# Turning two more batches of h on VectorE, moving their weights' low parts to GpSimd, and longer rows for the expert loads

## The chip, the cores and the metric

The kernel runs on one core of one Trainium2 chip. The metric is the device time of one execution in microseconds (us). The core has five engines with a queue each: TensorE (PE; its weight loads are listed apart as PEld), VectorE (DVE), ScalarE (ACT), GpSimd (POOL) and SyncE (SP), which issues all DMAs here. An engine takes its own queue in order.

## The reference, cut to what matters

Attention with normalised q and k feeds a gated feed-forward layer, and that feeds a soft mixture of experts. There are 4 batches of 448 tokens, 12 heads of 64, model width 768, hidden width 1536, 8 experts with 4 slots each and expert width 1024.

```
q_n, k_n = rmsnorm(q, g_q), rmsnorm(k, g_k)
attn = softmax(q_n @ k_n.T / 8);  x = (attn @ v), heads side by side        # 1792 x 768
h = silu(x @ w_gate) * (x @ w_val);  x2 = h @ w_out
logits = x2 @ phi                                   # 32 slots
slot_input = softmax over tokens(logits).T @ x2
slot_out[e] = relu(slot_input[e] @ w1[e]) @ w2[e]   # 8 experts, 50.3 MB of weights
out = softmax over slots(logits) @ slot_out
```

The kernel never forms x2. It uses w_out @ phi for the logits, and sums h over tokens with the slots' weights before it multiplies by w_out. For that sum h is needed with tokens on the partitions, while the feed-forward layer leaves it with hidden units on the partitions: each block of h (128 hidden units by 448 tokens) has to be turned. That turning is the subject here.

## The kernel before, in words

The program is a row of steps t. Steps 0 to 27 do the attention of batch 0 and prepare w_out @ phi. From step 28 on, u = t - 28 counts units of the feed-forward layer: 24 units for each batch, an even unit for a gate block and the odd one after it for the matching value block, 12 blocks of h a batch. Beside the units of batches 0, 1 and 2 run the scores and softmax of the attention of a later batch, four steps c = 0 to 3 for a pair of heads (three steps with two score tiles, the fourth with one). The units of batch 3 (u = 72 to 95) run without attention. Behind them come the slots' sums, the experts and the output.

Within a step the work is issued in the order of a table of names: ORD1 (line 1303) for batch 0, ORD2 (line 1306) for all later steps. Each engine gets its instructions in that order. The names that matter here, with the lines of the profile:

- S: scores of this step (L442, L446). M0, M1: their maxima on VectorE (L457). E0, E1: exponentials on ScalarE (L469). N0: the reciprocals of their sums on VectorE (L481, L482). N1, N2: scaling by them on GpSimd (L486). P0, P1: four transposes each of the step before's probabilities on TensorE (L521), and V0, V1 their copies out of PSUM (L535, L537). X: probabilities times v (L548). T, TH, L: transposes of the next q or k (L372), and their high and low parts (L403, L405, L414, L62). Q: on GpSimd the powers and products that normalise q and k (L340, L341, L347).
- G0, G1: the two halves of unit u, 9 matmuls each (L615), from a weight's high part wh and low part wl and x's high and low parts. WH makes wh of unit u+1 on ScalarE (L231); WL makes wl of unit u+1 by a subtraction (L239), in `w_lo`.
- AT, AM: the gate's and the value's activation (L629 on ScalarE, L636 and L642 on VectorE), which give the block ht of h.
- HT (`h_trans`, lines 658 to 674): turns a block by four TensorE transposes (L666) and one ScalarE copy (L670) into hn. Token chunks are 4 of 112 (`tok`, line 644). H0 to H3 (`h_squares`, lines 679 to 690): turn a block by 16 VectorE transposes of 32 by 32 squares (L685), four for each quarter of the block, H0 and H1 in the step after the block's value unit, H2 and H3 one step later. Here the chunks are 128, 128, 128 and 64 tokens, and the last chunk's lower half is set to zero by a GpSimd memset (L655). Before the change batches 0 to 2 use HT, and batch 3 uses H0 to H3.
- Z1, Z2, Z3, Z4: the slots' part of a finished batch, with the sums over h (`slots4`, L782) at u = 26, 50 and 74.

The low parts wl are made on VectorE for units 0 to 71 and on GpSimd (W4) for batch 3. The expert weights come in 32 units of 1.5 MB (`load_unit`): from u = 73 on, one load at every other step, and the rest behind the steps, each when its buffer comes free. Where a buffer is two half tiles, a unit is loaded in pieces (L940).

Of the kernel before, what the change touches and what calls it, by code (L numbers as in the profile page):

```python
# [21 lines left out]
def attn_moe_softmoe_kernel(  # L22
# [15 lines left out]
    nc = tc.nc  # L38
    B, H, S, HD = q.shape
    NT, DM = out.shape  # L40
    DFF = w_out.shape[0]
    NS = phi.shape[1]
    E, _, F = w1.shape
    SPE = NS // E
    P = 128
    CP = 112
    NC = S // CP
# [3 lines left out]
    KH = F // P  # L51
# [33 lines left out]
    ident = cpool.tile([P, P], F32, name="ident")  # L85
# [557 lines left out]

    def tok(b):

        return [P] * (S // P) + [S % P] if b == B - 1 else [CP] * NC

    def hn_tile(u):
        b, r = divmod(u, NU)
        g, f4 = divmod(r // 2, 4)  # L650
        d = bt[b]
        if g not in d["hn"]:
            d["hn"][g] = hnp.tile([P, NC, 512], F32, tag="hn", name="hn", bufs=3)
            if b == B - 1:
                nc.gpsimd.memset(d["hn"][g][S % P :, NC - 1], 0.0)  # L655
        return d["hn"][g], P * f4

    def h_trans(u, ht=None):

        b, r = divmod(u, NU)  # L660
        hn, o = hn_tile(u)
        ht = bt[b]["ht"][r // 2] if ht is None else ht
        th4 = pt_tile("th4")
        t0 = 0
        for c, n in enumerate(tok(b)):
            nc.tensor.transpose(th4[:n, P * c : P * c + P], ht[:, t0 : t0 + n], ident)  # L666
            t0 += n
        th4 = th4.rearrange("p (c f) -> p c f", c=NC)
        if b < B - 1:
            nc.scalar.copy(out=hn[:CP, :, o : o + P], in_=th4[:CP])  # L670
        else:
            n = S % P
            nc.scalar.copy(out=hn[:, : NC - 1, o : o + P], in_=th4[:, : NC - 1])
            nc.vector.tensor_copy(out=hn[:n, NC - 1, o : o + P], in_=th4[:n, NC - 1])

    SQ = 32
    hts_ = {}

    def h_squares(u, g):
# [76 lines left out]
    def slots3(b):  # L756
        d = bt[b]
        dp = pt_tile("dp")
        d["dn"] = mp.tile([P, NC, NS], F32, tag="dn", name="dn", bufs=1)
        if b == B - 1:  # L760
            nc.gpsimd.memset(d["dn"][S % P :, NC - 1], 0.0)

        for n, (src, dst, ck) in enumerate(((d["et"], d["dn"], tok(b)), (d["lr"], ce[:, b], [CP] * NC))):
            o = dp[:, NC * NS * n : NC * NS * (n + 1)].rearrange("p (c s) -> p c s", c=NC)
            t0 = 0
            for c, m in enumerate(ck):
                nc.tensor.transpose(o[:m, c], src[:NS, t0 : t0 + m], ident[:NS, :NS])
                t0 += m
            if n == 0 and b == B - 1:
                nc.vector.tensor_copy(out=dst[:, : NC - 1], in_=o[:, : NC - 1])  # L770
                nc.vector.tensor_copy(out=dst[: ck[-1], NC - 1], in_=o[: ck[-1], NC - 1])
            elif b < B - 1:
                nc.vector.tensor_copy(out=dst[:CP], in_=o[:CP])
            else:
                nc.scalar.copy(out=dst[:CP], in_=o[:CP])

    def slots4_mul(b, g):
        d = bt[b]
        sp = pt_tile("sp")
        n = P if b == B - 1 else CP  # L780
        for c in range(NC):
            nc.tensor.matmul(  # L782
                sp[NS * c : NS * c + NS, :], d["dn"][:n, c, :], d["hn"][g][:n, c, :], start=True, stop=True
            )
        return sp
# [135 lines left out]
    def load_unit(u):  # L921
        if u >= NE:
            return
        e, i, n = eunits[u]
        if i == 0:
            w, src = F, w1[e, KD2 * P * n : KD2 * P * (n + 1)].rearrange("(c p) f -> p c f", p=P)
        elif i == 1:
            w, src = DM, w2[e, KH2 * P * n : KH2 * P * (n + 1)].rearrange("(c p) f -> p c f", p=P)
        else:
            w, src = DM // 2, w2[e, :, DM // 2 * n : DM // 2 * (n + 1)].rearrange("(c p) f -> p c f", p=P)  # L930
        t = unit_tile(u)
        if isinstance(t, list):
            hf = KD2 * F // 2
            wtile[u] = lambda c, o, m: t[(c * w + o) // hf][:, (c * w + o) % hf : (c * w + o) % hf + m]
            for h in range(2):
                o = hf * h
                while o < hf * (h + 1):
                    c, lo = divmod(o, w)
                    m = min(w - lo, hf * (h + 1) - o)
                    nc.sync.dma_start(out=t[h][:, o - hf * h : o - hf * h + m], in_=src[:, c, lo : lo + m])  # L940
                    o += m
            return
        t = t.rearrange("p (c f) -> p c f", f=w)
        wtile[u] = lambda c, o, m: t[:, c, o : o + m]
        if u < NE - 1:
            nc.sync.dma_start(out=t, in_=src)
        else:
            for c in range(0, KH, 2):
                nc.sync.dma_start(out=t[:, c : c + 2], in_=src[:, c : c + 2])


    M0 = NP * NC + 4
# [2 lines left out]
    def wu(u):  # L955
        return NO + u if 0 <= u < B * NU else None
# [146 lines left out]
    def step(t):  # L1103
# [102 lines left out]

        def WL():
            if u + 1 < last:
                w_lo(wu(u + 1), nc.gpsimd if u + 1 < NU and WL1 == "p" else nc.vector)

        def M_(j):
            if att:
# [47 lines left out]
        def HT():  # L1260
            if prev is not None and prev % 2 == 1:
                if prev == B * NU - 1:
                    fill(LF[3])
                    slots1(B - 1)
                elif prev < (B - 1) * NU:
                    h_trans(prev)

        def H_(g):

            w = prev if g < 2 else u - 2  # L1270
            if w is not None and (B - 1) * NU <= w < B * NU - 1 and w % 2 == 1:
                if g == 0:
                    hts_[w] = bt[w // NU]["ht"][w % NU // 2]
                h_squares(w, g)
# [28 lines left out]
        "AT NB Z3 X W4 S NC XM NA SP T AM WH P0 Z1 TH G0 M0 M1 L WL E0 CT E1 N0 P1 XH R0 Z4 V1 HT N1 V0 XL N2 C SS G1 LG Q R Z2"  # L1303
    ).split()
    ORD2 = (
        "H2 H3 X S NB Z3 T AT NC M0 AM XM XH TH W4 M1 Z4 XL P0 V0 E0 L SP WH G0 NA Z1 CT E1 HT H0 H1 N0 R0 Z2 N1 N2 SS P1 G1 WL R LG V1 Q C"
    ).split()
    LF = [4, 3, 2, 0]
    LRE = 'v'
# [93 lines left out]
    with tc.manual_schedule():  # L1403
# [14 lines left out]
        sit_ps = pt_tile("sit")  # L1418
        for c in range(KD):
            nc.tensor.matmul(  # L1420
                sit_ps[:, NS * c : NS * c + NS], si[:, P * c : P * c + P], stack[:, 0, :], start=True, stop=True
            )
        sit = tp_.tile([P, KD, NS], F32, name="sit")
        nc.vector.tensor_copy(out=sit, in_=sit_ps[:, : KD * NS].rearrange("p (c s) -> p c s", c=KD))
# [34 lines left out]
        for u, (e, i, n) in enumerate(eunits):  # L1459
            w = wtile.pop(u)  # L1460
            if i == 0:
                if n == 0:
                    hacc[e] = s_tile(e % 3)[:, :FQ]
                for c in range(KD2 * n, KD2 * n + KD2):
                    for j in range(4):
                        nc.tensor.matmul(  # L1466
                            hacc[e][NS * j : NS * j + NS, :],
                            sit[:, c, :],
                            w(c % KD2, FQ * j, FQ),
                            start=(c == 0),  # L1470
                            stop=(c == KD - 1),
                        )
                if n == 1:

                    h1m = tp_.tile([P, KH, NS], F32, tag="h1m", name="h1m", bufs=2)
                    nc.gpsimd.memset(h1m, 0.0)
                    hr = tp_.tile([P, FQ], F32, tag="hr", name="hr", bufs=2)
                    nc.scalar.activation(out=hr, in_=hacc.pop(e), func=AF.Relu)
                    ht_ = pt_tile("htp")
                    for t in range(2):  # L1480
                        nc.tensor.transpose(ht_[:, P * t : P * t + P], hr[:, P * t : P * t + P], ident)
                    for t in range(2):
                        nc.vector.tensor_copy(
                            out=h1m.rearrange("p (j t) s -> p t j s", t=2)[:, t, :, SPE * e : SPE * e + SPE],
                            in_=ht_[:, P * t : P * t + P].rearrange("p (j s) -> p j s", j=4)[
                                :, :, SPE * e : SPE * e + SPE
                            ],
                        )
                    h1s[e] = h1m
            else:  # L1490
                for kh_ in range(KH2 * n, KH2 * n + KH2) if i == 1 else range(KH):
                    for j in range(4) if i == 1 else (2 * n, 2 * n + 1):
                        nc.tensor.matmul(  # L1493
                            so[NS * j : NS * j + NS, :],
                            h1s[e][:, kh_, :],
                            w(kh_ % KH2, DQ * j, DQ) if i == 1 else w(kh_, DQ * (j - 2 * n), DQ),
                            start=(e == 0 and kh_ == 0),
                            stop=(e == E - 1 and kh_ == KH - 1),
                        )
# [51 lines left out]
```

## Time and profile before

| | us |
|---|---|
| median of 3 runs | 825.45 (822.0 to 825.55) |
| the profiled execution | 825.7 |
| its span, first to last instruction | 823.9 |

The profiled execution is 0.25 us over the median. Beside the span lie 1.8 us. TensorE is busy 95% of the span, VectorE 59%, ScalarE 53%, GpSimd 47%. On the chain that ended last TensorE holds 85% and DMA 6%. Busy time shows what an engine does, and only the waits and the chain show whether it holds the others up; a busy TensorE is also not TensorE at its peak.

### The profile page before, as it was taken

The page shows a single profiled execution, that of the slowest core. Times are in us where ns is not written, and L with a number is a line of the kernel's source. Part 1 is how long each engine was busy: PE and PEld are TensorE (multiplying, and loading weights), DVE is VectorE, ACT ScalarE, POOL GpSimd, SP SyncE. Part 2 cuts the span into 40 slices and gives each one's busy share as a digit, 9 for nine tenths or more (in the row PEclk, how much of TensorE's full clock was granted, in tenths as well). Part 3 has the DMA queues.
Part 4 walks back from the last instruction along what each step waited for, and adds up shares of the span by engine and source line. Part 5 has one row for each costly group of instructions (what it writes and reads, how often), then busy time and mean ns, then how long its engine had stood idle before and what let it go on. Part 6 is the DMA issues. An engine that isn't in the chain of part 4 may idle for free.

```text
span 823.9 us, 14472 instructions
## 1 busy us (share of the span) xinstructions
PE 781.5 (95%) x5440; PEld 584.0 (71%) x5440; DVE 484.7 (59%) x943; ACT 434.8 (53%) x943; POOL 386.7 (47%) x354
## 2 busy tenths in 40 slices
PE   6899999999999999999999999999999999888676
PEld 5556657787778767877778677877878888555344
DVE  4879988777778555545555655544348778410013
ACT  3767887787778546655557465554432222211013
POOL 7988876665756444655355346422133445010000
PEclk8999999999999999999999999999999999999878
DMA  6556766675666312323232122221227888899998
GB/s 216 161 163 210 216 208 191 221 227 177 194 194 208 116 63 81 91 70 97 75 111 92 51 80 82 75 71 58 69 89 238 298 303 326 275 389 403 402 378 262
DMA packets 77892, 148.88 MB, mean 181 GB/s; under 512 B 5888, under 2 KB 48128, under 8 KB 77824
## 3 DMA queue, kind: packets, MB, share of 16 engines
q1 hardware_dynamic: 77824, 147.97, 53.9%
q8 instruction: 43, 0.70, 0.4%
q14 instruction: 25, 0.20, 0.1%
HBM read 128.29 MB, written 19.66 MB: 180 GB/s over the span
## 4 chain that ended last, share of the span: by engine, by line
PE 85%; DMA 6%; POOL 2%; ACT 2%; DVE 2%; issue 1%; SPq 0%; DVEq 0%; POOLq 0%; ACTq 0%
PE pg L615 43%; PE tp L521 9%; PE xp L548 7%; PE s L442 6%; DMA w<-in_moe_w_dram 6%; PE tq L372 3%; PE s L548 2%; PE th L666 2%; PE so L1493 2%; PE s L446 2%; PE lp L709 2%; PE sp L782 1%; PE s L1466 1%; PE s L1450 1%; PE tw L247 1%
## 5 line engine op out<-in xcount | busy, mean ns | idle before, releaser
L615 PE MATMUL pg<-xh,wh 128*128 128x448 f32 x576 | 224.1, 389 | 0.1
L615 PE MATMUL pg<-xl,wh 128*128 128x448 f32 x576 | 210.6, 366 | 0.0
L615 PE MATMUL pg<-xh,wl 128*128 128x448 f32 x432 | 157.6, 365 | 0.0
L457 DVE TENSOR_REDUCE sm<-s 128x1 f32<-128x448 f32 x168 | 100.7, 619 | 83.4 <-PE s L442 67.6
L486 POOL TENSOR_SCALAR pr<-pr,su 128x448 f32<-128x448 f32 x84 | 80.4, 966 | 139.9 <-ACT pt L535 62.5
L615 PEld LDWEIGHTS pg<-xh,wh 128*128 128x128 f32 x576 | 108.5, 188 | 15.3 <-issue 7.9
L615 PEld LDWEIGHTS pg<-xl,wh 128*128 128x128 f32 x576 | 108.8, 189 | 6.6 <-issue 0.2
L469 ACT ACTIVATE pr<-s,sm 128x448 f32<-128x448 f32 x168 | 107.6, 643 | 11.0 <-DVE sm L457 10.8
L535 ACT COPY pt<-tp 112x512 f32<-112x512 f32 x130 | 75.4, 590 | 66.0 <-PE tp L521 59.9
L521 PE MATMUL tp<-ident,pr 128*112 128x128 f32 x672 | 103.6, 277 | 2.5 <-ACT pt L535 1.8
L521 PEld LDWEIGHTS tp<-ident,pr 128*112 128x112 f32 x672 | 76.2, 134 | 29.3 <-issue 6.6
L231 ACT CAST wh<-raw 128x768 fp32r<-128x768 f32 x96 | 79.9, 835 | 23.8 <-POOL raw L239 23.6
L615 PEld LDWEIGHTS pg<-xh,wl 128*128 128x128 f32 x432 | 81.1, 188 | 6.7
L239 DVE TENSOR_TENSOR wl<-raw,wh 128x768 fp32r<-128x768 f32 x72 | 74.4, 1034 | 8.3 <-ACT wh L231 8.3
L239 POOL TENSOR_TENSOR raw<-raw,wh 128x768 fp32r<-128x768 f32 x24 | 44.2, 1842 | 69.3 <-ACT wh L231 67.1
L341 POOL TENSOR_TENSOR ri<-ss,mhalf 112x16 f32<-112x16 f32 (+1 forms) x25 | 72.8, 2911 | 2.1
L442 PE MATMUL s<-ka,qa 64*128 64x448 f32 x432 | 64.7, 404 | 0.8 <-ACT qa L403 0.7
L629 ACT ACTIVATE ht<-pg 128x448 f32<-128x448 f32 x48 | 26.1, 544 | 70.9 <-PE pg L615 45.9
L347 POOL TENSOR_TENSOR qn<-qk,ri 112x512 f32<-112x512 f32 x46 | 59.1, 1286 | 1.1
L548 PE MATMUL xp<-pt,vt 112*64 112x448 f32 x288 | 58.1, 545 | 0.0
L442 PEld LDWEIGHTS s<-ka,qa 64*128 64x128 f32 x432 | 35.5, 187 | 27.3 <-issue 24.3
L615 PE MATMUL pg<-xh,raw 128*128 128x448 f32 x144 | 52.8, 366 | 0.0
(162 smaller groups left out, 1153.0 us busy)
## 6 DMA issues: line engine op xcount, KB each, us to landing
w<-in_moe_w_dram SPq DMA_DIRECT2D x25, 1536.0 KB, 10.3
raw<-w SPq DMA_DIRECT2D x72, 384.0 KB, 3.2
w<-raw SPq DMA_DIRECT2D x36, 384.0 KB, 2.9
r<-in_moe_w_out_dram SPq DMA_DIRECT2D x12, 768.0 KB, 4.9
r<-in_moe_w_gate_dram SPq DMA_DIRECT2D x12, 768.0 KB, 5.1
r<-in_moe_w_val_dram SPq DMA_DIRECT2D x12, 768.0 KB, 5.1
qk<-in_q_dram SPq DMA_DIRECT2D x24, 224.0 KB, 2.9
qk<-in_k_dram SPq DMA_DIRECT2D x24, 224.0 KB, 3.2
```

Source lines behind the costliest of these rows:

```text
L231: (nc.vector.tensor_copy if u - NO < NU and WH1 == "v" else nc.scalar.copy)(out=wh, in_=wst[u]["raw"])
L239: eng.tensor_tensor(out=wl, in0=wst[u]["raw"], in1=wst[u]["wh"].bitcast(F32), op=ALU.subtract)
L341: nc.gpsimd.tensor_tensor(out=ri, in0=ss, in1=mhalf[:, : len(ns)], op=ALU.pow)
L347: eng.tensor_tensor(out=st[i]["qn"][:, n].rearrange("p c h d -> p h c d"), in0=st[i]["qk"][:, n], in1=st[i]["ri"][:, n] .rearrange("p (h c ...
L442: nc.tensor.matmul(sc[j], qa[r, wt, c * P : (c + 1) * P], ka[r, mv, :], start=(n == 0), stop=(n == 2))
L457: nc.vector.tensor_reduce(out=d["sm"][:, j : j + 1], in_=d["sc"][j], axis=AX.X, op=ALU.max, negate=True)
L469: nc.scalar.activation(out=p, in_=d["sc"][j], func=AF.Exp, bias=d["sm"][:, j : j + 1], accum_out=st[i]["su"][:, c, j : j + 1])
L486: nc.gpsimd.tensor_scalar(out=p, in0=p, scalar1=su[:, j : j + 1], scalar2=1.0, op0=ALU.mult, op1=ALU.mult)
L521: nc.tensor.transpose(tp[:CP, ck * P : (ck + 1) * P], pr[:, ck * CP : (ck + 1) * CP], ident)
L535: eng(out=st[i]["pt"][j][:, :, c * P : (c + 1) * P], in_=tp)
L548: nc.tensor.matmul(xp[HD * j : HD * j + HD, :S], d["vt"][:, j, ck, :], d["pt"][j][:, ck, :], start=(ck == 0), stop=(ck == NC - 1),)
L615: nc.tensor.matmul(d[r], wt[:, P * c : P * c + P], mv, start=(c == 0 and n == 0), stop=(c == KD - 1 and n == 2),)
```

## The change

Four edits. `SQB` is B - 3 = 1.

- Batches 1 and 2 are turned like batch 3: H0 to H3 in place of HT, with chunks of 128, 128, 128 and 64 tokens, and a memset for each of their hn tiles and the dn tile.
- The low parts wl of the units of batches 1 and 2 are made on GpSimd in place of VectorE.
- Expert loads: a partition takes 3 neighbouring rows of w1 (12288 bytes in one piece) in place of 3 pieces of 4096 bytes, or 2 neighbouring rows of w2 (6144 bytes) in place of pieces of 3072 bytes. Half tiles take 6144 bytes a partition. The last four units (halves of w2's columns, 1536 bytes a piece) keep their pieces, but all four, and not only the last, are issued in four parts of 384 KB. To match, the slots' sums (si) and the experts' hidden values (hr) are read with strides of 3 and 2 elements by the transposes.
- A new ORD2.

```diff
-        return [P] * (S // P) + [S % P] if b == B - 1 else [CP] * NC
+        return [P] * (S // P) + [S % P] if b >= SQB else [CP] * NC
...
-            if b == B - 1:
+            if b >= SQB:
                 nc.gpsimd.memset(d["hn"][g][S % P :, NC - 1], 0.0)
...
-    SQ = 32
+    SQ, SQB = 32, B - 3
...
-            w, src = F, w1[e, KD2 * P * n : KD2 * P * (n + 1)].rearrange("(c p) f -> p c f", p=P)
+            w, src = F, w1[e, KD2 * P * n : KD2 * P * (n + 1)].rearrange("(m p c) f -> p m (c f)", m=1, p=P)
         elif i == 1:
-            w, src = DM, w2[e, KH2 * P * n : KH2 * P * (n + 1)].rearrange("(c p) f -> p c f", p=P)
+            w, src = DM, w2[e, KH2 * P * n : KH2 * P * (n + 1)].rearrange("(m p k) f -> p m (k f)", p=P, k=2)
         else:
-            w, src = DM // 2, w2[e, :, DM // 2 * n : DM // 2 * (n + 1)].rearrange("(c p) f -> p c f", p=P)
+            w, src = DM // 2, w2[e, :, DM // 2 * n : DM // 2 * (n + 1)].rearrange("(m p k) f -> p m k f", p=P, k=2)
...
-                w_lo(wu(u + 1), nc.gpsimd if u + 1 < NU and WL1 == "p" else nc.vector)
+                w_lo(wu(u + 1), nc.gpsimd if u + 1 >= SQB * NU else nc.vector)
...
-                elif prev < (B - 1) * NU:
+                elif prev < SQB * NU:
                     h_trans(prev)
...
-            if w is not None and (B - 1) * NU <= w < B * NU - 1 and w % 2 == 1:
+            if w is not None and SQB * NU <= w < B * NU - 1 and w % 2 == 1:
...
-        "H2 H3 X S NB Z3 T AT NC M0 AM XM XH TH W4 M1 Z4 XL P0 V0 E0 L SP WH G0 NA Z1 CT E1 HT H0 H1 N0 R0 Z2 N1 N2 SS P1 G1 WL R LG V1 Q C"
+        "NB S R0 SS AT X WH NC T XM Z3 W4 AM XH TH M1 Z4 H0 M0 E0 XL H2 H1 SP L E1 Q H3 G0 P0 WL Z1 HT Z2 N0 G1 N2 NA CT P1 V1 LG R V0 N1 C"
...
-                sit_ps[:, NS * c : NS * c + NS], si[:, P * c : P * c + P], stack[:, 0, :], start=True, stop=True
+                si[:, KD2 * P * (c // KD2) : KD2 * P * (c // KD2 + 1)].rearrange("q (p c) -> q c p", c=KD2)[:, c % KD2],
...
-                        nc.tensor.transpose(ht_[:, P * t : P * t + P], hr[:, P * t : P * t + P], ident)
+                            ht_[:, P * t : P * t + P], hr.rearrange("q (p t) -> q t p", t=2)[:, t], ident
```

On TensorE, in a step c = 2 of batch 1 (scores s, transposed probabilities tp, unit pg, turned block th; nine pg rows make one half), before:

```order
L442 MATMUL s<-ka,qa 128x448 x6
L521 MATMUL tp<-ident,pr 112x128 x4
L615 MATMUL pg<-xh,wh 128x448
...
L666 MATMUL th_4131<-ident,ht 112x128 x4
L521 MATMUL tp<-ident,pr 112x128 x4
L615 MATMUL pg<-xh,wh 128x448
...
```

And the same step now:

```order
L442 MATMUL s<-ka,qa 128x448 x6
L615 MATMUL pg<-xh,wh 128x448
...
L521 MATMUL tp<-ident,pr 112x128 x4
L615 MATMUL pg<-xh,wh 128x448
...
L521 MATMUL tp<-ident,pr 112x128 x4
```

The four transposes of the h block are gone, and each set of transposed probabilities stands behind a half unit in place of ahead of it.

On GpSimd, the four steps of one pair of heads in batch 1 (qz is a copy of q's last columns, pr the probabilities, ri and qn the normalising, wl the low part), before:

```order
L423 COPY qz_110<-qa 64x2x64 x2
L486 TENSOR_SCALAR pr<-pr,su 128x448 x4
L340 TENSOR_SCALAR ss<-ss 112x16
L341 TENSOR_TENSOR ri<-ss,mhalf 112x16
L486 TENSOR_SCALAR pr<-pr,su 128x448 x2
L347 TENSOR_TENSOR qn<-qk,ri 112x2x4x64
L486 TENSOR_SCALAR pr<-pr,su 128x448
L347 TENSOR_TENSOR qn<-qk,ri 112x2x4x64
```

And now:

```order
L423 COPY qz_110<-qa 64x2x64 x2
L239 TENSOR_TENSOR wl<-raw,wh 128x768
L486 TENSOR_SCALAR pr<-pr,su 128x448 x2
L340 TENSOR_SCALAR ss<-ss 112x16
L341 TENSOR_TENSOR ri<-ss,mhalf 112x16
L239 TENSOR_TENSOR wl<-raw,wh 128x768
L486 TENSOR_SCALAR pr<-pr,su 128x448 x2
L347 TENSOR_TENSOR qn<-qk,ri 112x2x4x64
L239 TENSOR_TENSOR wl<-raw,wh 128x768
L486 TENSOR_SCALAR pr<-pr,su 128x448 x2
...
```

Four subtractions came in, each ahead of its step's scalings, and the power of step c = 1 (ri) and the products (qn) stand ahead of the subtraction.

On VectorE, the step c = 2 now (maxima sm, activation ht, squares hn, reciprocals su); before, neither the squares nor anything else stood between its two maxima but the activation, and a subtraction wl stood at its end:

```order
L642 SCALAR_TENSOR_TENSOR ht<-ht,pg 128x448
L457 TENSOR_REDUCE sm<-s 128x1
L685 STREAM_TRANSPOSE hn<-ht 32x4x32 x2
L685 STREAM_TRANSPOSE hn<-ht 32x3x32 x2
L457 TENSOR_REDUCE sm<-s 128x1
L685 STREAM_TRANSPOSE hn<-ht 32x4x32 x2
L685 STREAM_TRANSPOSE hn<-ht 32x3x32 x2
L481 TENSOR_SCALAR su<-su 128x2
L482 RECIPROCAL su<-su 128x2
```

Eight squares came in at this step, four of them between the two maxima.

## Rows read from the trace of the kernel before

**Rows 1.** The page, engines: busy us, share of the span, instructions.

```profile
PE 781.5 (95%) x5440; PEld 584.0 (71%) x5440; DVE 484.7 (59%) x943; ACT 434.8 (53%) x943; POOL 386.7 (47%) x354
```

**Rows 2.** Stretches: length, busy us (instructions) of PE, PEld, DVE, ACT, POOL; clock; DMA.

```profile
304.00:467.00 163.00, 162.24 (x975) 125.86 (x967) 90.48 (x174) 95.58 (x207) 81.40 (x79) 1.00 0.28 84
467.00:612.00 145.00, 144.99 (x849) 113.91 (x848) 70.59 (x132) 76.91 (x163) 50.19 (x51) 1.00 0.24 73
740.00:760.00 20.00, 17.82 (x334) 11.66 (x338) 0.77 (x6) 2.70 (x6) 1.79 (x5) 1.00 1.03 405
788.00:800.00 12.00, 9.27 (x96) 6.00 (x90) 0.61 (x3) 0.38 (x1) 0.00 (x0) 0.85 1.06 373
```

**Rows 3.** Waits of PE from 304 to 612 us: total, times, longest.

```profile
PE dp L767 <- DVE dn L773: 0.8, 1, 0.8
```

**Rows 4.** Chain in batch 1, order of time: start, us, what.

```profile
349.52 3.16 PE xp L548 x16
352.68 0.81 PE s L442 x6
353.48 0.53 PE tq L372 x4
...
354.45 1.83 PE pg L615 x9
...
361.77 0.44 PE th L666 x4
...
375.50 3.16 PE xp L548 x16
```

**Rows 5.** Groups from 304 to 612 us: busy us, mean ns; idle before.

```profile
L486 POOL TENSOR_SCALAR pr<-pr,su 128x448 f32<-128x448 f32 x73 | 70.4, 973 | 122.9 <-ACT pt L535 62.5 <-ACT hn L670 30.3 <-DVE su L482 30.0
L239 DVE TENSOR_TENSOR wl<-raw,wh 128x768 fp32r<-128x768 f32 x45 | 46.0, 1022 | 8.3 <-ACT wh L231 8.3
L457 DVE TENSOR_REDUCE sm<-s 128x1 f32<-128x448 f32 x73 | 45.4, 622 | 74.3 <-PE s L442 59.7 <-PE s L446 14.5
L341 POOL TENSOR_TENSOR ri<-ss,mhalf 112x16 f32<-112x16 f32 x9 | 26.3, 2919 | 0.8
L642 DVE SCALAR_TENSOR_TENSOR ht<-ht,pg 128x448 f32<-128x448 f32 x24 | 14.7, 612 | 4.9 <-PE pg L615 4.9
L327 DVE TENSOR_REDUCE ss<-qn 112x16 f32<-112x1024 f32 x8 | 9.6, 1199 | 0.0
L481 DVE TENSOR_SCALAR su<-su 128x2 f32<-128x2 f32 (+1 forms) x42 | 7.0, 167 | 44.6 <-ACT pr L469 44.6
L414 DVE SCALAR_TENSOR_TENSOR qa<-tq,gsc,qa 128x448 fp32r<-128x448 f32 x9 | 6.1, 676 | 0.0
L423 POOL CAST qz<-qa 64x128 fp32r<-64x128 f32 x18 | 5.2, 288 | 28.5 <-DVE qa L414 28.0
```

**Rows 6.** Single lines, whole trace: ns shortest/median/longest, first and last start.

```profile
L685 DVE STREAM_TRANSPOSE hn<-ht x176: 269/284/305, 619.1 to 706.1; 32x128 f32<-32x128 f32 x88, 32x96 f32<-32x96 f32 x88
L239 POOL TENSOR_TENSOR raw<-raw,wh x24: 1818/1842/1856, 602.4 to 699.2; 128x768 fp32r<-128x768 f32 x24
L486 POOL TENSOR_SCALAR pr<-pr,su x84: 628/639/2287, 264.0 to 583.0; 128x448 f32<-128x448 f32 x84
L347 POOL TENSOR_TENSOR qn<-qk,ri x46: 1035/1044/1812, 15.7 to 531.5; 112x512 f32<-112x512 f32 x46
```

**Rows 7.** Chain in the experts' part: start, us, what.

```profile
747.74 20.35 DMA w<-in_moe_w_dram
...
776.12 19.94 DMA w<-in_moe_w_dram
```

**Rows 8.** SyncE's queue, DMA issues in order of time: start, us, line, count.

```profile
716.66 2.46 SPq L940 DMA_DIRECT2D w<-in_moe_w_dram  x4
721.17 27.01 SPq L946 DMA_DIRECT2D w<-in_moe_w_dram  x11
```

**Rows 9.** SyncE's waits: total, times, longest.

```profile
SPq L940 <- PE sp L782: 9.6, 2, 8.9
```

More of the change, by code (lines that the diff above doesn't have):

```diff
@@ L668, in h_trans @@
         th4 = th4.rearrange("p (c f) -> p c f", c=NC)
-        if b < B - 1:
+        if b < SQB:
             nc.scalar.copy(out=hn[:CP, :, o : o + P], in_=th4[:CP])
@@ L759, in slots3 @@
         d["dn"] = mp.tile([P, NC, NS], F32, tag="dn", name="dn", bufs=1)
-        if b == B - 1:
+        if b >= SQB:
             nc.gpsimd.memset(d["dn"][S % P :, NC - 1], 0.0)
@@ L768, in slots3 @@
                 t0 += m
-            if n == 0 and b == B - 1:
+            if n == 0 and b >= SQB:
                 nc.vector.tensor_copy(out=dst[:, : NC - 1], in_=o[:, : NC - 1])
@@ L779, in slots4_mul @@
         sp = pt_tile("sp")
-        n = P if b == B - 1 else CP
+        n = P if b >= SQB else CP
         for c in range(NC):
@@ L935, in load_unit @@
             for h in range(2):
[L936 to L941, printed above, removed]
+                nc.sync.dma_start(out=t[h], in_=src[:, h] if i else src[:, 0, hf * h : hf * (h + 1)])
             return
[L943 to L946, printed above, removed]
-        else:
-            for c in range(0, KH, 2):
-                nc.sync.dma_start(out=t[:, c : c + 2], in_=src[:, c : c + 2])
+        tv = t.rearrange("p (c f) -> p c f", f=w)
+        wtile[u] = lambda c, o, m: tv[:, c, o : o + m]
+        if i < 2:
+            nc.sync.dma_start(out=t.rearrange("p (m f) -> p m f", m=i + 1), in_=src)
+        else:
+            for m in range(KH // 2):
+                nc.sync.dma_start(out=tv[:, 2 * m : 2 * m + 2], in_=src[:, m])
     M0 = NP * NC + 4
@@ L1420, in attn_moe_softmoe_kernel @@
             nc.tensor.matmul(
-                sit_ps[:, NS * c : NS * c + NS], si[:, P * c : P * c + P], stack[:, 0, :], start=True, stop=True
+                sit_ps[:, NS * c : NS * c + NS],
+                si[:, KD2 * P * (c // KD2) : KD2 * P * (c // KD2 + 1)].rearrange("q (p c) -> q c p", c=KD2)[:, c % KD2],
+                stack[:, 0, :],
+                start=True,
+                stop=True,
             )
@@ L1480, in attn_moe_softmoe_kernel @@
                     for t in range(2):
-                        nc.tensor.transpose(ht_[:, P * t : P * t + P], hr[:, P * t : P * t + P], ident)
+                        nc.tensor.transpose(
+                            ht_[:, P * t : P * t + P], hr.rearrange("q (p t) -> q t p", t=2)[:, t], ident
+                        )
                     for t in range(2):
```

## The prediction

> **What bounds the kernel now.** I read the engines' totals first: TensorE is busy 95% of the span [rows 1]. A total says nothing of the stages, so the stretches come next: in batches 1 and 2, from 304 to 612 us, TensorE is busy 307.2 of 308 us, while VectorE has 161.1 (52%) and GpSimd 131.6 (43%) [rows 2]. The list of waits shows that this is a bound and not only a busy engine: in those 308 us TensorE waits once, 0.8 us [rows 3]. The chain of waits agrees: it runs from one TensorE piece to the next without a gap [rows 4]. So there each TensorE instruction that goes is worth its time, and work given to VectorE or GpSimd is free until TensorE has to wait for it. The experts' part is another matter: the chain runs through loads of expert weights (20.35 and 19.94 us in its two longest pieces [rows 7]), the DMA engines are full (share 1.03) at 405 GB/s, and TensorE's waits there cost nothing more [rows 2].
>
> **The turned blocks.** 24 blocks (12 in each of batches 1 and 2) lose four transposes, 0.44 us on the chain [rows 4]: 24 x 0.44 = 10.6 us less on TensorE. ScalarE loses 24 copies, which matters to nobody.
>
> VectorE gains 24 x 16 = 384 squares of 0.284 us [rows 6], 109 us, and loses 48 subtractions of 1.02 us, 49 us [rows 5]: 161 + 60 = 221 us in some 297, or 74%. Over the four steps of a pair of heads: 32 squares 9.1, seven maxima 4.4, four activations 2.4, the low parts of q, k and x (three at 0.62 to 0.68) 1.9, one sum of squares 1.2, four sums made safe and inverted, twice 0.167 each [rows 5], 1.3, and 0.3 for the logits, 20.6 us. TensorE's four steps take 375.50 - 349.52 = 25.98 us [rows 4], less two blocks of 0.44, 25.1 us. So VectorE has 4.5 us to spare.
>
> GpSimd gains 48 subtractions of 1.842 us [rows 6], 88 us. But a scaling there takes 0.639 us in the median and 0.973 us on the mean of these batches, with one of 2.287, and a product of qn 1.044 in the median, 1.812 at worst [rows 5, 6]: something lengthens it. VectorE's subtractions, the only big VectorE operation there with two inputs from SBUF, are the suspect, and they leave. The Trainium skill ("SBUF — State Buffer", Who interferes with whom) says that a VectorE instruction with two SBUF inputs and a GpSimd one that reads SBUF block each other; by it the short durations hold after the change, without it the long ones. GpSimd's four steps: two qz 0.6, four subtractions 7.4, seven scalings 4.5, power and its scale 3.1, two products 2.1, 17.7 us of 25.1. With the long durations it would be 20.7.
>
> **Where lateness would come from.** Both engines fit on average; what decides is the order. Tightest is this: in step c = 0 VectorE does the sum of squares (1.20), an activation (0.61), two maxima (1.24), eight squares (2.27) and q's low part (0.68), together 6.0 us. Behind that GpSimd copies qz (0.6, at 6.6), makes wl (8.4), scales twice (9.7), does the power of c = 1 (12.8) and the next wl (14.7 us). TensorE reads that last wl after steps c = 0 (0.81 + 0.53 + 1.83 + 0.44 + 1.83 = 5.4) and c = 1 (the same, and 3.16 for X and 0.44 more, 9.0), another 0.81 of scores and two matmuls of 0.2: at 15.7 us. The slack is 1.0 us, once in four steps. The scalings of step c = 1 end at 16.0, and TensorE wants their results only after the first half unit, at 17.1. The scores' buffers are free in time, since the exponentials come right behind the maxima.
>
> Twice, at u = 26 and 50, there is a new wait: the memset of hn (L655) waits until the sums of the batch before have read that buffer, behind it stand the products, wl and the scalings on GpSimd, and behind the squares one maximum on VectorE. That step is some 3.5 us longer on TensorE by those sums, which covers most of it. No row shows this wait with attention beside it. Bounds: nothing, and 2 us each, since eight squares (2.3 us) are what it can push; I take 0.5 each, 1.0 in all, nearer to nothing because rows 3 show TensorE waiting 0.8 us in all at the two such places now.
>
> **The rest of the order.** The other moves on TensorE change no instruction, and TensorE has no gaps to win. I cost them at nothing, covered by the same slack; without it, the rival below. ORD2 also runs batch 3, where no attention competes and GpSimd already makes wl.
>
> **The loads.** What shortens batches 1 and 2 moves the experts too: expert loads begin at u = 73 in SyncE's order and wait at 707 to 717 us for the last sums on TensorE (8.9 us [rows 9]). So the 10.6 us carry to the end. Behind that pause, from 716.66 us [rows 8], 21 units remain (32 less 11 issued earlier), 17 of them with changed rows: 17 x 1.573 MB = 26.7 MB. Pieces of 1536 bytes move at 373 GB/s, those of 4096 and 3072 bytes mixed at 405 [rows 2]. Taking a fixed time a piece: 1536 bytes take 4.12 ns (all engines together), 3511 bytes (the harmonic mean of 4096 and 3072) 8.67 ns; 1975 bytes more cost 4.55 ns, which is 434 GB/s and 0.58 ns a piece. Pieces of 12288 and 6144 bytes (mean 8192) then take 19.5 ns, an estimate of 421 GB/s: 26.7 MB in 63.4 us in place of 65.9, 2.5 us less. Bounds: a piece that costs nothing, 434 GB/s, 4.4 us less; and at worst the rate of the 1536 byte pieces, if long pieces spread unevenly over the engines, 5.7 us more. I take 2.5: the two rows nearest to it rise with length.
>
> The Trainium skill ("DMA: Bandwidth & Descriptors", Specifications) says that from 512 bytes on a transfer runs at line rate. By that all these pieces are alike, and the sum would be 2.5 us higher. This trace does not agree: at a full share 373 stands against 405 GB/s, with both lengths above it.
>
> The strided reads of si and hr touch 12 and 16 weight loads of 0.16 to 0.19 us; were each twice as long, 5 us, beside loads on which the end hangs. The 16 part loads in place of 7 for the last four units cost SyncE about 0.4 us each while the engines have work queued. Both at nothing; uncovered, the last unit's share is under 1 us.
>
> Sum, against the profiled execution: 825.7 - 10.6 + 1.0 - 2.5 = 813.6 us. It stands 0.25 over the median, so I forecast 813.5.
>
> **The rivals.**
> *Long rows bring nothing:* the rate stays at 405. For it: GB/s at full share hardly tells 4096 from 3072 in these rows. Against: 373 at 1536. 825.7 - 10.6 + 1.0 = 816.1.
> *The slack goes:* wl or the scalings come about 1 us late once in four steps, 12 times: 12 us return, 825.6. For it: 1.0 us is a thin slack, and VectorE at 82% of its four steps often starts one late. Against: TensorE's present order has hardly a wait [rows 3], and a late step also gives the next one more time.
> *Slower:* GpSimd's chain at c = 0 and c = 1 holds TensorE each time. VectorE enters c = 0 with eight squares still queued (2.3 us), and scalings stay at 0.973 (0.7 us more): 14.7 + 3.0 = 17.7 against 15.7, 2.0 us late, 12 times 24 us: 825.7 - 10.6 - 2.5 + 24 = 836.6. It decides from a lateness of 1.4 us (12 x 1.4 covers the 12.1 gained and 4 more). For it: squares and subtractions both enter this chain. Against: the relief of GpSimd, and 4.5 us spare on VectorE in each four steps.
> *The end doesn't move:* loads keep their own pace from some fixed point, and only the rows count, 823. Against: SyncE issues them in the steps' order and waits for TensorE [rows 8, 9].
> That the change doesn't do what it says is excluded by the order of the instructions, except for the rows' rate, the first rival.
>
> **How the numbers follow.** The forecast with its own bounds (4.4 less on loads and no waits, 810.7; 4 us of waits and 1 us lost on loads, 820) gets 0.68, long rows without effect 0.12, the slack gone or the end unmoved 0.10, slower 0.07, and 0.03 below 810. The range is 808.5 to 822.5: it leaves out the last of the third case, the slower one and a little below. What a measurement can tell from no change is about 0.5%, 4.1 us: faster means under 821.3 (0.82), the same up to 829.6 (0.10), slower above (0.08).
>
> **What would show it.** Right: TensorE still without waits in batches 1 and 2, which take some 10 us less; no L666 there; scalings near 0.64 us on the mean; squares near 0.28; the load stretch at about 420 GB/s. Wrong: TensorE waiting for wl (L239 on GpSimd) or pr (L486), most of all at c = 2; scalings still near 0.97; the rate at 405 or under; or loads that begin as late as now.

## The result, and the profile after

The changed kernel takes **815.32 us** (median of 4 runs, 814.67 to 816.17), against 825.25 us for the kernel before in the same rounds: a ratio of 0.9884, 95% interval 0.9871 to 0.9898. Forecast were 813.5 us, range 808.5 to 822.5. The profiled execution took 814.67 us, its span 812.9, 11.0 less than before.

The page's engine line (busy us, share, instructions), which answers to [rows 1]:

```profile
PE 771.0 (95%) x5344; PEld 576.8 (71%) x5344; DVE 555.7 (68%) x1281; ACT 422.8 (52%) x919; POOL 443.9 (55%) x410
```

TensorE lost 96 instructions, the four transposes of 24 blocks, and 10.5 us of busy time. The stretches that answer to [rows 2] (length; busy us and instructions of PE, PEld, DVE, ACT, POOL; clock; DMA share; GB/s):

```profile
304.00:467.00 163.00, 161.98 (x953) 124.27 (x946) 130.35 (x351) 89.43 (x195) 109.19 (x109) 1.00 0.27 84
467.00:612.00 145.00, 142.32 (x810) 110.48 (x809) 106.70 (x305) 71.69 (x154) 77.99 (x75) 1.00 0.26 78
740.00:760.00 20.00, 17.30 (x338) 11.29 (x334) 0.77 (x6) 1.15 (x3) 0.94 (x3) 1.00 1.01 418
```

VectorE went from 161.1 to 237.1 us in the two batches (77% of 308; forecast 74%), and the loads from 405 to 418 GB/s (forecast 421). TensorE now misses 3.7 us in place of 0.8. The waits of PE from 304 to 612 us (total, times, longest), in place of the one line of [rows 3]:

```profile
PE dp L767 <- DVE dn L771: 1.3, 2, 0.8
PE pg L615 <- DVE xl L62: 1.1, 1, 1.1
PE dp L767 <- ACT et L746: 0.7, 1, 0.7
PE dp L767 <- DVE su L481: 0.4, 1, 0.4
```

None is for wl or pr, and all lie where a batch ends: 0.9 us ahead of the sums behind batch 1 (0.8 before) and 2.6 at the end of batch 2 (0.6 before, at 615 us). So TensorE "without waits in batches 1 and 2", a sign of the prediction, holds inside the batches and not at the end of the second. The chain at the end of batch 2 (start, us, what) shows how:

```profile
596.40 0.30 DVE hn L685
...
598.81 0.64 DVE xl L62
...
599.49 1.28 PE pg L615 x5
...
605.04 0.28 DVE hn L685
...
605.34 0.64 DVE sml L739
...
608.19 0.40 PE dp L767 x4
608.59 2.71 PE sp L782 x24
```

Eight squares (596.40 to 598.78) stand ahead of x's low part on VectorE, and eight more (602.92 to 605.31) ahead of the logits' maximum; TensorE waits behind both. Before, HT had given VectorE nothing there.

To see where the time was won, each batch is measured between two groups of 24 matmuls (`sp`, L782): from the last start in the sums of the batch before to the first start in its own:

| us | before | after |
|---|---|---|
| first sums of batch 0 start | 303.8 | 302.7 |
| batch 1 | 161.2 | 156.9 |
| batch 2 | 146.2 | 143.9 |
| batch 3 | 96.8 | 94.9 |
| the sums behind batches 0 / 1 / 2 / 3, first to last start | 2.2 / 2.2 / 2.2 / 3.1 | 2.2 / 2.8 / 2.2 / 4.3 |
| loads go on behind the pause (SyncE) | 716.66 | 707.63 |

So batches 1 and 2 gave 4.3 and 2.3 us, not 5.3 each; batch 3, whose operations are the same, gave 2.0 (96.83 - 94.85) that nobody had forecast. The earlier start of the first sums, 1.1 us, is no gain: in eleven other kernels they start anywhere from 302.2 to 305.3, but from the first matmul of unit 0, ahead of which nothing was changed, they all take 177.7 to 177.9 us. From the pause on, 9.0 became 11.0.

The sums behind batch 1 last 0.65 us longer. A wait of the weight loads shows why (PEld, total, times, longest):

```profile
PEld sp L782 <- POOL dn L761: 0.5, 1, 0.5
```

The change has dn's lower half set to zero there too, and this memset stands on GpSimd behind two scalings (460.95 to 462.20 us) and starts at 462.26, after the first sums had started. In the kernel "one batch" below, which has no such memset behind batch 1, the sums take 2.2 us again.

One cycle of four steps in batch 1, from X to X, shows a part of why it is 4.3 and not 5.3. The chain after, against [rows 4]:

```profile
347.70 3.16 PE xp L548 x16
...
361.06 0.45 PE tp L521 x4
...
363.09 0.62 DVE ht L636
363.71 0.53 DVE sm L457
...
366.98 1.22 DVE ss L327
368.20 0.53 DVE ht L642
368.72 0.54 DVE sm L457
...
370.36 0.64 DVE sm L457
...
372.36 0.55 ACT pt L537 x2
...
372.95 1.34 PE xp L548 x5
```

The cycle takes 25.3 us from first matmul to first matmul (347.63 to 372.95; before 25.98, forecast 25.1). VectorE is busy 19.9 of them (forecast 20.6). From 363.09 to 370.99 us the chain runs on VectorE with no more than 0.05 us between two instructions: activation, maxima, eight squares, the sum of squares and four more squares, and then by the softmax to the X that ends the cycle. TensorE has work in the meantime and shows no wait there, but X's first weight load stands idle until pt arrives, and X starts 0.95 us behind the scores in place of 0.80. From 304 to 612 us this happens at four of eleven X:

```profile
PEld xp L548 <- ACT pt L537: 1.7, 4, 0.5
```

On this piece of the cycle VectorE has nothing to spare, whatever it has over all four steps.

GpSimd's groups from 304 to 612 us (busy us, mean ns; idle before), against [rows 5]:

```profile
L239 POOL TENSOR_TENSOR wl<-raw,wh 128x768 fp32r<-128x768 f32 x45 | 82.6, 1835 | 12.7 <-ACT wh L231 11.7
L486 POOL TENSOR_SCALAR pr<-pr,su 128x448 f32<-128x448 f32 x73 | 45.9, 639 | 43.3 <-DVE su L482 34.0 <-ACT pt L535 3.1 <-PE tp L521 2.2
L347 POOL TENSOR_TENSOR qn<-qk,ri 112x512 f32<-112x512 f32 x18 | 18.8, 1045 | 0.4
```

The squares take 0.286 us on the mean (forecast 0.284). The scalings fell from a mean of 973 to 639 ns, the products from 1392 (25.1 us for 18 in the kernel before) to 1045. And the thin slack of the prediction (timeline: start, us, engine, line):

```profile
353.95 1.84 POOL L239 TENSOR_TENSOR wl<-raw,wh 128x768 fp32r<-128x768 f32 x1
357.20 0.36 PE L615 MATMUL pg<-xh,wl 128*128 128x448 f32 x1
```

wl is done at 355.79 and read at 357.20, 1.4 us later (forecast 1.0).

### The profile page after: what moved, and what is told of

Same layout as the page of the kernel before. It is cut to its first block, busy times and chain, and to the rows that moved or that the text cites. A ratio compares the mean times of both kernels' runs of the same rounds, so it can differ in the third digit from the quotient of the medians.

```text
span 812.9 us, 14547 instructions
## 1 busy us (share of the span) xinstructions
PE 771.0 (95%) x5344; PEld 576.8 (71%) x5344; DVE 555.7 (68%) x1281; ACT 422.8 (52%) x919; POOL 443.9 (55%) x410
## 4 chain that ended last, share of the span: by engine, by line
PE 80%; DVE 6%; DMA 5%; ACT 3%; POOL 2%; issue 1%; SPq 0%; DVEq 0%; POOLq 0%; ACTq 0%
PE pg L615 40%; PE tp L521 8%; PE xp L548 7%; PE s L442 6%; DMA w<-in_moe_w_dram 5%; PE tq L372 3%; PE s L548 2%; DVE hn L685 2%; PE so L1495 2%; PE sp L782 2%; PE lp L709 2%; PE s L446 1%; PE s L1466 1%; DVE sm L457 1%; PE s L1450 1%
## 5 line engine op out<-in xcount | busy, mean ns | idle before, releaser
L685 DVE STREAM_TRANSPOSE hn<-ht 32x128 f32<-32x128 f32 (+1 forms) x560 | 160.1, 286 | 8.8
L535 ACT COPY pt<-tp 112x512 f32<-112x512 f32 x130 | 71.9, 589 | 69.0 <-PE tp L521 62.9
L239 POOL TENSOR_TENSOR wl<-raw,wh 128x768 fp32r<-128x768 f32 x48 | 88.1, 1836 | 13.7 <-ACT wh L231 12.7
L486 POOL TENSOR_SCALAR pr<-pr,su 128x448 f32<-128x448 f32 x84 | 54.3, 657 | 53.6 <-DVE su L482 41.4
L636 DVE SCALAR_TENSOR_TENSOR ht<-ht,pg 128x448 f32<-128x448 f32 x48 | 29.6, 618 | 41.6 <-ACT ht L629 41.5
L423 POOL CAST qz<-qa 64x128 fp32r<-64x128 f32 x48 | 24.4, 509 | 58.2 <-DVE qa L414 32.2
```

Source lines behind the costliest of these rows:

```text
L239: eng.tensor_tensor(out=wl, in0=wst[u]["raw"], in1=wst[u]["wh"].bitcast(F32), op=ALU.subtract)
L486: nc.gpsimd.tensor_scalar(out=p, in0=p, scalar1=su[:, j : j + 1], scalar2=1.0, op0=ALU.mult, op1=ALU.mult)
L535: eng(out=st[i]["pt"][j][:, :, c * P : (c + 1) * P], in_=tp)
L685: nc.vector.transpose(out=hn[SQ * k : SQ * k + SQ, :m, o + SQ * g : o + SQ * g + SQ], in_=hk.rearrange("p (c q) -> p c q", q=SQ)[:, k :: P ...
```

## The experiments

Ratios are to the kernel before in the same rounds; its median in them was 827.12 us for the first four experiments and 824.2 to 824.9 for the others, so gains are taken from the ratios. "Batch" is the measure of the table above.

**Rows alone.** Before, with only the new loads and strided reads.

```diff
-    w, src = F, w1[e, ...].rearrange("(c p) f -> p c f", p=P)
+    w, src = F, w1[e, ...].rearrange("(m p c) f -> p m (c f)", m=1, p=P)
...
```

> The kernel before with only the longer rows of the expert loads (and the strided reads of si and hr that go with them). Theory (a piece has a fixed cost, so longer pieces move faster): 2 to 2.5 us less than before, 822.5 to 823.3, with the load stretch near 420 GB/s in place of 405. Rival (all pieces above 512 bytes move alike): 825.3, no change. Second rival (the strided weight loads cost the chain 0.75 us at sit and 0.1 us at each expert): 826 to 827, slower.

Measured: 823.22 us, ratio 0.9953 (0.9934 to 0.9972), 3.9 us less; batches 161.2, 146.2, 96.6 as before. Its stretch:

```profile
740.00:760.00 20.00, 16.96 (x294) 10.71 (x294) 0.81 (x7) 3.28 (x7) 3.53 (x8) 1.00 1.02 422
```

422 GB/s: the rows raise the rate by themselves. This kernel also issues all of the last four units in four parts; no run has the one without the other.

**All but the rows.** After, with the loads and reads of before (the diff above, reversed).

> The changed kernel with the loads of before (pieces of 4096 and 3072 bytes) and plain reads of si and hr; squares, subtractions on GpSimd and new order stay. Theory: 2 to 2.5 us slower than the changed kernel, 817.3 to 817.8, and the loads still begin 9 us earlier than before. Rival (rows bring nothing): 815.3. If the sum of this run's and the rows-only run's gains falls short of 10 us, the two parts help each other.

Measured: 820.1 us, ratio 0.9905 (0.9881 to 0.9928); batches 156.9, 143.9, 95.3 as in the changed kernel; 402 GB/s:

```profile
740.00:760.00 20.00, 17.30 (x333) 10.82 (x326) 0.77 (x6) 1.69 (x4) 0.94 (x3) 1.00 1.03 402
```

The rate shows the rows' part from this side too. In time they are worth 3.9 us alone and 1.7 (0.0021 of 825) on the changed kernel, the forecast 2.5 between. But the 1.7 is the difference of two ratios whose intervals overlap (0.9871 to 0.9898 for the changed kernel), and can't be told from nothing.

**Order alone.** Before, with the new ORD2.

```diff
-        "H2 H3 X S NB Z3 T ... WH G0 NA Z1 CT E1 HT H0 H1 N0 R0 Z2 N1 N2 SS P1 G1 WL R LG V1 Q C"
+        "NB S R0 SS AT X WH NC T XM Z3 ... H3 G0 P0 WL Z1 HT Z2 N0 G1 N2 NA CT P1 V1 LG R V0 N1 C"
```

> The kernel before with only the new ORD2: batches 1 and 2 are turned by TensorE, the low parts are made on VectorE, old loads. Theory (the gain is TensorE's transposes that are gone): all 24 sets of transposes stay on the chain, so at most the 2.0 us that batch 3 gained and the 1.1 us ahead of batch 1 come back: 822 to 825.5. Rival (the order is the gain, and what leaves TensorE is hidden): 818 or less, with batches 1 and 2 shorter by 5 us or more.

Measured: 825.21 us, ratio 0.9978 (0.9964 to 0.9991); batches 161.2, 146.6, **94.9**: nothing won in batches 1 and 2 (0.4 lost in the second), and batch 3 as short as in the changed kernel. And GpSimd's scalings, with the subtractions still on VectorE:

```profile
L486 POOL TENSOR_SCALAR pr<-pr,su 128x448 f32<-128x448 f32 x73 | 46.1, 643 | 147.9 <-DVE su L482 133.1 <-ACT pt L535 8.2 <-ACT hn L670 5.7
```

So the scalings' relief doesn't need the subtractions to leave VectorE. It needs them not to run at the same time: in the trace of the kernel before 41 of these 73 scalings overlap a subtraction and take 1236 ns on the mean, and the other 32 take 636, none over 646. Here none overlaps one.

**All but the order.** After, with the old ORD2.

> The changed kernel with the old ORD2: squares, subtractions on GpSimd and longer rows stay. Theory (TensorE's time is what counts, the order only keeps lateness away): the 10.6 us of transposes stay away, but in the old order the probabilities are wanted a half unit earlier and the squares stand ahead of the maxima, so TensorE waits for pr: between 817 and 826, with named waits of TensorE for pr or wl in batches 1 and 2. Rival 1 (slack is wide, order indifferent): 815 to 817, no such waits. Rival 2 (the squares need the new order): 826 or more, the change would be a loss without it.

Measured: 841.25 us, ratio 1.0181 (1.0158 to 1.0204); batches 168.4, 151.1. TensorE's waits from 304 to 612 us, and the chain at c = 0 to c = 2 of a pair of heads:

```profile
PE pg L615 <- POOL wl L239: 15.1, 20, 1.3
```

```profile
359.99 0.18 DVE su L481
...
360.55 1.26 POOL pr L486 x2
361.81 1.80 POOL wl L239
...
363.99 2.91 POOL ri L341
...
367.58 1.26 POOL pr L486 x2
368.84 1.79 POOL wl L239
...
370.68 1.47 PE pg L615 x6
```

My theory (817 to 826 us) was wrong, and its second rival right. This is the prediction's slower rival, step by step: reciprocals, scalings, wl, power, scalings, wl, and TensorE at its end; only its long scalings are missing (two take 1.26 us). Squares and subtractions under the old order are slower than the kernel before. The order, which I had costed at nothing, is worth some 25 us to them.

**wl behind the scalings.** After, with WL moved behind N1.

```diff
-... H3 G0 P0 WL Z1 HT Z2 N0 G1 N2 NA CT P1 V1 LG R V0 N1 C
+... H3 G0 P0 Z1 HT Z2 N0 G1 N2 NA CT P1 V1 LG R V0 N1 WL C
```

> The changed kernel with one name of the new ORD2 moved: WL (the subtraction that makes wl on GpSimd) behind N1, so that it stands behind its step's scalings, as in the old order. Theory (what the old order loses is that wl waits behind scalings, which wait for the whole softmax of the step): at c = 1 the scalings end 1.7 us after wl ends now and wl another 1.84 later, about 2 us too late, in one to three of four steps: 15 to 45 us slower than the changed kernel, 830 to 860, TensorE waiting for wl (L239) by name. Rival (the old order loses by the place of the squares ahead of the maxima or of the transposes ahead of the half unit): no more than 3 us slower, under 819.

Measured: 857.27 us, ratio 1.0395 (1.0374 to 1.0416); batches 180.7, 161.6; from 304 to 612 us:

```profile
PE pg L615 <- POOL wl L239: 25.5, 18, 2.1
```

As expected: that one place is worth 42 us in the new order.

**wl early in the old order.** The old ORD2, with WL moved right behind G0.

```diff
-... SP WH G0 NA Z1 CT E1 HT H0 H1 N0 R0 Z2 N1 N2 SS P1 G1 WL R LG V1 Q C
+... SP WH G0 WL NA Z1 CT E1 HT H0 H1 N0 R0 Z2 N1 N2 SS P1 G1 R LG V1 Q C
```

> The old ORD2 with squares, subtractions on GpSimd and longer rows, and WL alone moved ahead, right behind G0 and ahead of the scalings. Theory: most of the 26 us between old and new order come back: 816 to 826, few waits for wl left; what stays comes from pr, wanted ahead of the first half unit. Rival (squares ahead of the maxima, or transposes first, are the cause): 836 or more, as with the whole old order.

Measured: 836.08 us, ratio 1.0128 (1.0107 to 1.0149); batches 168.3, 151.4, as with the old order untouched. My expectation was wrong. The total is 4 us under the old order's, none of it in the batches. wl is in time, and TensorE waits for the scalings instead, as long as it had for wl:

```profile
PE tp L521 <- POOL pr L486: 15.8, 17, 1.7
```

So wl's place is not the whole of the order. The old table puts the transposes of pr ahead of a half unit, and scalings come late to them once GpSimd has the subtractions ahead.

**Slack, more than there is.** After, with 20 small memsets on GpSimd ahead of wl at c = 1, 11 times.

```diff
+            if c == 1 and NU <= u < last and att:
+                for _ in range(20):
+                    nc.gpsimd.memset(scr, 0.0)
```

> The changed kernel with 20 small memsets more on GpSimd (0.11 us each, 2.2 us together) ahead of wl in each step c = 1 of batches 1 and 2, eleven times; nothing reads them. Theory (wl at c = 1 has 1.0 us of slack by the prediction, 1.4 us by the trace after: it ends at 355.79, TensorE reads it at 357.20): late by 0.8 to 1.2 us eleven times, 9 to 13 us slower, 824 to 828. Rival (GpSimd at two thirds of its time has room on average, so nothing is late): under 818. Rival 2 (the chain was at its limit all along): 838 or more, all 24 us on the clock.

Measured: 840.69 us, ratio 1.0198 (1.018 to 1.0217), some 26 over the changed kernel. The 20 memsets take more than I had reckoned, since they start 167 ns apart (timeline; lines count one higher in this kernel):

```profile
359.61 3.33 POOL L1207 MEMSET scr<- 128x16 f32 x20
362.95 1.80 POOL L240 TENSOR_TENSOR wl<-raw,wh 128x768 fp32r<-128x768 f32 x1
```

11 x (3.33 - 1.4) = 21 us; batches 1 and 2 are 17.7 and 6.2 longer, 23.9, or 2.17 us a time. If what goes past the slack comes back whole, the slack is 3.33 - 2.17 = 1.2 us on the mean. The total is that of my second rival (838 or more), but by memsets half as long again as I had put them, and not for want of any slack.

**Slack, a little less than there is.** The same with 8 memsets.

> The changed kernel with 8 memsets (128x16) on GpSimd ahead of the low part at each c = 1 step of batches 1 and 2, 11 times. By the 20 memsets that lasted 3.33 us, 8 last 1.33 us, against a slack of 1.4 us between the end of wl and its first reader. Theory (a lateness within the slack costs nothing): not over 817 us, TensorE waits for wl of no more than 2 us in all. Rival (there is no slack on average, every microsecond on GpSimd is one on TensorE): 11 x 1.33 = 14.6 us more, 830 us.

Measured: 821.2 us, ratio 0.9957 (0.9943 to 0.9971), 6 us over the changed kernel: between both theories. The memsets took 1.29 us:

```profile
355.84 1.29 POOL L1207 MEMSET scr<- 128x16 f32 x8
```

Waits for wl are 2.1 us, 4 times, against 2 at most by the theory, but batches 1 and 2 are 3.7 and 0.9 longer, 0.42 us a time on 11, which leaves a slack of 1.29 - 0.42 = 0.9 us on the mean. The 1.4 us of the cycle that I had measured isn't that of every cycle. Another 1.7 us lie in the sums behind batch 1, told below.

**Subtractions on VectorE.** After, with wl of units 24 to 71 left on VectorE.

```diff
-                w_lo(wu(u + 1), nc.gpsimd if u + 1 >= SQB * NU else nc.vector)
+                w_lo(wu(u + 1), nc.vector)
```

> The changed kernel with the 48 low parts of weights left on VectorE (squares and new order kept). Theory (the subtractions had to leave VectorE): its four steps take 20.6 + 4 x 1.02 = 24.7 of TensorE's 25.25 us, so it cannot make up any lateness, and the squares and maxima behind a subtraction come late: 822 to 840 us, TensorE waiting for VectorE by name in 304 to 612 us. Also scalings on GpSimd stay near 0.97 us on the mean if VectorE's subtractions lengthen them. Rival (half a microsecond to spare is enough with this order, and GpSimd's relief outweighs it): 813 to 818 us, and scalings at 0.64.

Measured: 821.69 us, ratio 0.9957 (0.9939 to 0.9975), 6 over the changed kernel and just under what I expected; batches 160.5 and 146.1, close to before: the gain of the squares is gone. Its chain is the changed kernel's with one piece more:

```profile
367.39 0.27 DVE hn L685
...
367.70 0.96 DVE wl L239
...
368.84 1.22 DVE ss L327
370.06 0.53 DVE ht L642
...
374.82 1.34 PE xp L548 x5
```

The subtractions had to leave VectorE, at this place of the cycle. The scalings' mean is 643 ns here too; no scaling overlaps a subtraction in this order, so that part of the theory was wrong, as order alone had shown.

**One batch.** After, with batch 1's h turned by TensorE again, its wl still on GpSimd.

```diff
-    SQ, SQB = 32, B - 3
+    SQ, SQB = 32, B - 2
...
-                w_lo(wu(u + 1), nc.gpsimd if u + 1 >= SQB * NU else nc.vector)
+                w_lo(wu(u + 1), nc.gpsimd if u + 1 >= NU else nc.vector)
```

> The changed kernel with batch 1's h blocks turned by TensorE again (12 blocks, 5.3 us more TensorE work there); the low parts of batch 1 stay on GpSimd. Theory (0.44 us a block, TensorE the bound in batch 1): batch 1 takes 4.3 us longer than in the changed kernel, the end 818.5 to 820.5 us. Rival (the gain of batch 1 is from the order and from GpSimd's relief, not from the blocks): not over 817 us.

Measured: 817.92 us, ratio 0.9916 (0.99 to 0.9933); batches 161.2, 143.9, 94.3. Batch 1 is exactly that of before, 4.3 us longer than in the changed kernel, as expected; the total is 0.6 below what I expected, 2.6 us over the changed kernel by the ratios, in part since the sums behind batch 1 don't wait for dn's memset. The whole gain of batch 1 comes from its blocks, and none from GpSimd's relief.

**Something better?** After, with x's low part ahead of the squares (SP behind AM), the logits' pieces Z1 and Z2 ahead of M1 and H2, and both sets of dp transposed before their copies.

```diff
-... W4 AM XH TH M1 Z4 H0 M0 E0 XL H2 H1 SP L E1 Q H3 G0 P0 WL Z1 HT Z2 N0 ...
+... W4 AM SP XH TH Z1 M1 Z4 H0 M0 E0 XL Z2 H2 H1 L E1 Q H3 G0 P0 WL HT N0 ...
```

> The changed kernel with the waits taken away that its trace still shows where one batch follows another: SP (x's last parts for batch 3) ahead of the squares, Z1 and Z2 (logits' maxima and exponentials) ahead of squares and of the first half unit, and in slots3 both sets of transposes ahead of their copies. Theory (TensorE waits there 3.9 us in batches 1 and 2, and 0.8 us more at the last batch): 3 to 5 us faster than the changed kernel, 810 to 812.5. Rival (the other moves of order cost as much, or the loads' pace hides it): 814 to 817.

Measured: 814.06 us in the median, but 811.16 to 819.42 over six runs, ratio 0.9882 (0.9853 to 0.9912): not to be told from the changed kernel. The waits moved on (`PE sp L785 <- DVE dn L773: 1.7, 1, 1.7` among them) instead of going. Inconclusive.

## Why the prediction came out

*Turned blocks, 10.6 us less on TensorE.* Right as a price: 10.5 us of busy time went. Of it 6.6 us arrived (4.3 + 2.3), where the prediction's sign of being right was some 10. The rest is in places that I had at nothing. Set against the order alone, unit by unit, each block gives 0.43 to 0.45 us. X's wait for pt takes 0.10 to 0.15 back, three times in batch 1 and once in batch 2. The waits ahead of the sums behind batch 1 are 0.85 us, with the order alone 0.4. At the end of batch 2 the squares stand ahead of x's low part and of the logits' maximum: 1.10 + 0.71 + 0.82 us of waits against 0.6 before and with the order alone, or 2.2 by the starts of the matmuls. That gives 5.3 - 0.4 - 0.5 = 4.4 for batch 1, measured 4.3; and 5.3 - 0.1 - 2.2 = 3.0 for batch 2, less the 0.4 that the new order costs it, 2.6, measured 2.3. The last 0.3 are not accounted for.

*VectorE has 4.5 us to spare.* True of four steps, and the wrong question: between 363 and 371 us it has none. The subtractions on VectorE showed what 0.96 us there costs.

*The memset waits, 1.0 us.* At u = 50 hn's memset waits 1.16 us for the sums, as I had said, and TensorE waits for nothing behind it. What TensorE did pay for is dn's memset, 0.65 us at the sums behind batch 1, which I had not looked at. The waits at the batches' ends, 2.1 us more than before, mostly have another cause, the squares. (I also read [rows 3] as holding both places; it holds u = 50 alone, and 0.4 us more lie at u = 26.)

*Slack 1.0 us.* Measured 1.4 in the cycle looked at, and 0.9 to 1.2 on the mean by the two kernels with memsets. These show the mechanism from both sides, though not as a clean threshold.

*The order at nothing.* The step that was mis-sized most, without harm to the sum: for the kernel before it wins nothing in batches 1 and 2 and most of 2.0 us in batch 3, but for the changed kernel it is what separates a ratio of 0.9884 from 1.0181. The slower rival was a true mechanism, held off by the place of wl and of the transposes of pr.

*GpSimd's relief.* Forecast and seen, with the reason half right. The Trainium skill ("SBUF — State Buffer", Who interferes with whom) has a VectorE instruction with two SBUF inputs contend with a GpSimd one that reads SBUF. In the trace of before a pair of scalings beside VectorE's subtraction took 1.78 us, and 1.25 after; order alone gave 643 ns on the mean with the subtractions still on VectorE. Every scaling over 646 ns overlaps a subtraction. The runs agree with that rule, and it is the overlap in time that counts. But one pair took 2.90 us in the trace of before, 1.65 more than without, beside a subtraction of 0.95: why it lost more than the whole of that stays open.

*Loads, 2.5 us.* 418 GB/s against 421 forecast; 9.0 at the pause became 11.0 at the end, and the two kernels give 3.9 us and 1.7, the latter within the noise. Right, as far as it can be told. The strided reads cost 0.75 us at the sums' product sit (2.29 in place of 1.54), while loads run; whether any of it reached the end isn't shown.

So the mechanism was right in the main, and the total came within 2 us in part by luck. At the pause 9.6 us were forecast (10.6 - 1.0). Batches 1 and 2 gave 6.6, the sums behind batch 1 took 0.65 back, and batch 3's 2.0, which I had at nothing, made it 7.9; the rest of the 9.0 is the earlier start ahead of unit 0. With 2.0 behind the pause in place of 2.5 that is 9.9 us, the difference of the medians (825.25 - 815.32), against 12.1 forecast.

## What to carry to other kernels

Busy time over a cycle says whether work fits on an engine. Whether it costs is decided by the longest piece of the chain that runs on that engine without a gap: look for it in the chain of waits before giving the engine more. When work goes to an in-order engine, try its place in the queue along with it; here the same edits are 10 us faster or 15 slower by the order alone, and curing one late operand only uncovered the next. And look at the ends of the loops apart, where the steps' usual cover is missing.

## What the runs showed of the hardware that was not expected

A short pause of TensorE can be followed by a slower stretch. In the kernel with 8 memsets, the sums behind batch 1 took 4.5 us from first to last start, and 2.8 in the changed kernel, for the same 24 matmuls and the same wait for dn's memset (stretches; columns as above):

```profile
464.00:467.00 3.00, 1.23 (x14) 0.73 (x14) 1.74 (x8) 2.11 (x6) 1.28 (x3) 1.00 0.64 208
467.00:470.00 3.00, 3.00 (x22) 1.28 (x17) 1.69 (x3) 0.00 (x0) 1.02 (x3) 0.55 0.00 0
```

TensorE was busy 1.23 of 3 us, and then had a mean granted clock of 0.55, for the most part the lower of its two levels (1.2 and 2.4 GHz). The changed kernel shows it at its last sums (0.50 from 704 to 708 us, behind 1.58 busy us of 4), and at none of its earlier ones; the kernel before, too, at its last (0.50 from 714 to 716 us, behind 1.48 of 4). The kernel with the better ends shows it behind batch 1 (0.50 from 462 to 464 us, behind 0.77 of 2), where its sums took 1.5 us longer than the changed kernel's. All but the rows and one batch show it behind batch 2 (0.50 from 612 to 614 and from 613 to 615 us). So in the profiled executions of these kernels 1.2 to 1.7 us lie in sums, outside the batches' measure.

Batch 3 became 2.0 us shorter with the same instructions and no named wait of TensorE in either kernel. Two things are mixed in it. First, four units take 15.66 us in the new order and 15.95 in the old where the matmuls of a unit start 0.2027 us apart, and 15.95 against 16.16 where they start 0.2067 apart: 0.2 to 0.3 us by the order, 1.3 to 1.7 in the 24 units. Second, the matmuls start at one of these two distances for units on end, at a granted clock of 1.00 in both. The kernel before has both, the changed kernel the shorter one; but with the subtractions left on VectorE it is the longer one throughout, with the order and the instructions of the changed kernel in batch 3, which takes 96.3 us there. So this part isn't the order's. Why there are two distances stays open.
